# Keys and queries fetched early into the second weight's tile, regrouped joins, more unread products in the chain, and the first MLP group in free order

## The chip, the cores and the metric

The kernel runs on one core of a Trainium2 chip. The metric is the time on the device in microseconds (us), the median of several runs. A smaller time is better. Everything is computed in float32. The names of the engines are those of the profile: PE is the tensor engine's matrix product, PEld its weight load, DVE the vector engine, ACT the scalar engine, POOL GpSimd, SP the sync engine, which here only issues transfers.

## The reference, cut to what matters

Two blocks follow each other. The first is a delta rule (a linear attention whose state is corrected at each position), for 4 batches of 8 heads, 768 positions, head size 48:

```python
k_n = k / (np.linalg.norm(k, axis=-1, keepdims=True) + 1e-06)
for t in range(S):
    y[:, :, t] = np.einsum('bhd,bhde->bhe', q[:, :, t], state)
    v_old = np.einsum('bhde,bhd->bhe', state, k_n[:, :, t])
    state = state + beta[:, :, t, None, None] * np.einsum(
        'bhd,bhe->bhde', k_n[:, :, t], v[:, :, t] - v_old)
```

Its output, with the heads laid side by side, is x: 4 x 768 x 384. The second block mixes by a Fourier transform over positions and over the model's width, and then applies an MLP:

```python
u = x + np.real(np.fft.fft(np.fft.fft(x, axis=1), axis=2))
un = (u - mean(u)) / np.sqrt(var(u) + 1e-06)
out = u + np.maximum(un @ w_ch1, 0.0) @ w_ch2      # 384 -> 1536 -> 384
```

The two weights arrive as float64, and the kernel turns them into float32 itself.

## The kernel before, in words

**The delta rule in chunks.** A group g is 128 positions of one batch, all 8 heads: six groups for a batch (NL), 24 in all. For the groups of a round (RL = 4 groups) the kernel makes the products of the keys with themselves (`pre_a`), and from them the inverse of a unit triangular matrix of 32 x 32, for all heads and blocks side by side on the 128 partitions. `invert` (line 313) does this on DVE: one transpose, some small operations for the norms, then for each of 31 columns a product (L372) and a sum (L376), and two transposes (L379, L380). The first two rounds use `invert16` (line 386), which inverts the blocks of 16 only; `join` (line 464) then adds the corner between two such blocks by two sets of small products on PE, the first for `G` by `Gc`, the second for `Y` by `A` and `A` by `Y`, with an ACT copy between them and two DVE sums after them (L485). `pre_q` (line 493) transposes the queries and multiplies them with the keys. `pre_m` (line 524) forms what a step needs (W and U0), and `step` (line 580) moves the state over 64 positions, two steps for a group. Steps depend on each other; everything else only prepares for them.

**The Fourier part** is `fourier` (line 660): it folds x to even and odd halves (L680 to L691, POOL and DVE), multiplies by the tables over the positions (`pf`, L701 copies them to F), and then, in six T steps, multiplies over the width (`pb`) and adds to x, with the mean and variance for the norm (L720 to L735). **The MLP** is `mlp` (line 741): three groups of 256 positions for a batch. For a group PE makes 12 tiles of `ph` (the first weight, three products each), which ACT or DVE take through the ReLU to hT (L762, L764), and then two tiles of `po` (the second weight, 12 products each), which DVE adds to x (L774). `mlp` is a generator; a unit of it is one `ph` tile or four `po` products.

**The weights.** `weights` (line 221) brings each weight in six pieces, as pairs of 32-bit words. A piece goes through ACT (L253, L261), five operations on DVE (L254 to L265) and a product on POOL (L268), which writes it into w1 or w2.

**Where data lives.** Keys in the layout of `pre_a` have three tiles C and, for groups 3 and 4, the two query tiles. `home` (line 141) says which. Keys 5 to 7 go to the C tiles again, so `pre_a` of groups 0 to 2 issues their transfers when it has read a tile (line 295). Queries have two tiles, `Qs`; `pre_a` of groups 3 and 4 issues the first two, and each `pre_q` issues the query two groups ahead once it has read its own (line 504). `load_beta` issues four small transfers on SP.

**What sets the order.** All of the first batch runs in a block with a hand order (`manual_schedule`): there each engine runs its instructions in the order in which the program writes them. Generators are advanced by hand: `advance(gen, n)` runs n of a generator's units, `drain` the rest. After that block the loop over batches goes on, and there a scheduler orders the instructions. In the block: the keys of the first eight groups, the first inversion, queries 1 to 3, the joins, and then the steps of the six groups, with joins, the second inversion and w1's pieces between (`fill`); then the Fourier part of batch 0, the first group of its MLP with w2's pieces (`conv`), then the third inversion's first instruction, `pre_q(6)` and the beginning of `pre_m(6)`. In the loop, for each later step, `beside` (from line 808) names what runs next to it: the next group's preparation, keys and inversion of the next round, and MLP units of the batch before.

**Unread products.** `spin(n)` (line 195) issues n products of a zero tile with itself, 128 x 128 x 128, into a PSUM tile that nothing reads. In float32 each is two records in the trace. They are there to keep PE busy. The tile of zeros is filled on DVE at the start.

Of the kernel before, what the change touches and what calls it, by code (L numbers as in the profile page):

```python
# [9 lines left out]
F32 = mybir.dt.float32  # L10
# [50 lines left out]
def kernel(  # L61
# [80 lines left out]
    def home(g):  # L142

        return Cs[g] if g < 3 else Qs[g - 3] if g < 5 else Cs[(g - 5) % 3]
# [4 lines left out]

    def load_q(g):  # L150
        if g < NLT:
            nc.sync.dma_start(out=Qs[g % 2][:, :, 0:D], in_=rows(q, g))
# [9 lines left out]
    def load_beta(r):  # L162
# [5 lines left out]
        while i < RL:  # L168
            b, n = divmod(RL * r + i, NL)
            m = min(RL - i, NL - n)  # L170
            for q4 in range(4):
# [4 lines left out]
                nc.sync.dma_start(out=t[p0:p0 + 8 * m], in_=src)  # L176
# [3 lines left out]
    pack = const.tile([128, 128 + C + 3], F32, name="pack")  # L180
    load_c(0)
    nc.scalar.dma_start(out=pack, in_=cn["pack"].ap())
    load_c(1, nc.scalar)
    load_c(2)
    load_c(3)
    load_c(4)
    load_beta(0)
# [19 lines left out]
    w2 = const.tile([128, KF, DM], F32, name="w2")  # L207
# [77 lines left out]
    def pre_a(g):  # L285
# [9 lines left out]
        if g < 3:  # L295
            load_c(g + 5)
        elif g < 5:
            load_q(g - 3)
        else:
            load_c(g + 3)  # L300
# [161 lines left out]
    def join(g):  # L462
# [14 lines left out]
        for m in range(8):  # L477
            for q4 in range(4):
                rw = slice(W * q4, W * q4 + W)
                mm(pm[rw, V16 * m:V16 * m + V16], Y[rw, m, :], MTd[rw, 8 * li + m, V16:W], m == 0)  # L480
                o = 8 * V16 + V16 * m
# [9 lines left out]
    def pre_q(g, QT=None, LQ=None):  # L491

        Q, KT = Qs[g % 2], KTs.pop(g)
# [10 lines left out]
        load_q(g + 2)  # L504
# [340 lines left out]
    with tc.manual_schedule(engines=engines):  # L845
        unread.append(ps_post([128, 512], "unread"))
        spin(18)
# [7 lines left out]
        for g in range(2 * RL):  # L855
            if g == RING:
                drain(qs[0])
            advance(keys[g])
            if g > 0:
                advance(keys[g - 1])  # L860
            if g == RL:
                advance(inv0, 3)
                load_kv(0, nc.gpsimd)
                load_beta(1)
        drain(keys[-1])
        advance(inv1)
        load_kv(1, nc.gpsimd)
        drain(inv0)
        load_kv(2)
# [4 lines left out]
        nc.sync.dma_start(out=dtab, in_=cn["dtab"].ap())  # L874
        for qg in qs[1:4]:
            spin(3)
            advance(qg)
            spin(3)
            drain(qg)
        spin(4)  # L880
# [7 lines left out]
        advance(js[0])  # L888
        advance(js[1])
        advance(inv1, 6)  # L890
        advance(js[2])
        advance(pms[0])
        advance(inv1, 6)
        advance(pms[1])
        advance(pms[0])
        advance(inv1, 6)
        advance(js[2])
        advance(inv1, 6)
        advance(pms[1])
# [15 lines left out]
        for g in range(NL):  # L915
# [5 lines left out]
            if g > 0:  # L921
                advance(s0)
                fill()
                advance(out_g)
# [4 lines left out]
            fill()  # L929
            if g == 1:  # L930
# [5 lines left out]
            spin(2)  # L936
            advance(s1)
            fill()
            advance(p2)
# [4 lines left out]
            if g < NL - 1:  # L944
                advance(s1)
                fill()
                advance(p1)
                for jg in jn:
                    advance(jg)
# [77 lines left out]
```

## Time and profile before

The median of three runs is 855.03 us (852.42 to 860.65); the profiled execution spans 849.1 us.

| What | us | Share |
|---|---|---|
| PE busy | 743.0 | 88% |
| PE weight load busy | 579.4 | 68% |
| DVE busy | 385.1 | 45% |
| ACT busy | 206.2 | 24% |
| POOL busy | 128.7 | 15% |
| `ph` products (864) | 219.3 | |
| `po` products (576) | 197.7 | |
| Mean granted clock of PE | 0.885 of full | |

A busy time is the sum of an engine's instructions in the trace. The share tells how full an engine is over the whole span, and hides that the stages differ. The granted clock is the share of full speed that PE was allowed. In a row of the timeline the first number is the start, the second the time from the first start to the last end of the records gathered in the row; the brackets at its end give the idle time ahead of it on its engine, and after the arrow what ended it. A row of a group of instructions has, after the number of records, the busy time in us and the mean ns of one, and then the idle time ahead of them.

### The profile page before, as it was taken

The page shows a single profiled execution, that of the slowest core. Times are in us where ns is not written, and L with a number is a line of the kernel's source. Part 1 is how long each engine was busy: PE and PEld are TensorE (multiplying, and loading weights), DVE is VectorE, ACT ScalarE, POOL GpSimd, SP SyncE. Part 2 cuts the span into 40 slices and gives each one's busy share as a digit, 9 for nine tenths or more (in the row PEclk, how much of TensorE's full clock was granted, in tenths as well). Part 3 has the DMA queues.
Part 4 walks back from the last instruction along what each step waited for, and adds up shares of the span by engine and source line. Part 5 has one row for each costly group of instructions (what it writes and reads, how often), then busy time and mean ns, then how long its engine had stood idle before and what let it go on. Part 6 is the DMA issues. An engine that isn't in the chain of part 4 may idle for free.

```text
span 849.1 us, 26492 instructions
## 1 busy us (share of the span) xinstructions
PE 743.0 (88%) x11988; PEld 579.4 (68%) x11988; DVE 385.1 (45%) x959; ACT 206.2 (24%) x478; POOL 128.7 (15%) x151
## 2 busy tenths in 40 slices
PE   7658888666579899979998999889999999999998
PEld 6547777555456676748885776767867767776775
DVE  1816444535579611992628812499412131421110
ACT  4213332242231332203331222212212211110010
POOL 3521222201230110112100112101100010000000
PEclk9665555597689999999999999999999999989999
DMA  7911323141212132111211122001111000000000
GB/s 108 221 27 33 70 67 101 25 113 37 77 45 59 28 60 51 36 22 30 53 33 37 40 38 50 14 4 34 30 34 30 2 21 1 19 1 19 5 15 19
DMA packets 107395, 36.28 MB, mean 43 GB/s; under 512 B 99633, under 2 KB 102930, under 8 KB 107282
## 3 DMA queue, kind: packets, MB, share of 16 engines
q1 hardware_dynamic: 105586, 33.50, 17.8%
q8 instruction: 94, 1.54, 0.8%
q0 software_dynamic: 512, 0.79, 0.5%
q10 hardware_dynamic: 1184, 0.30, 0.2%
q14 instruction: 19, 0.16, 0.1%
HBM read 29.84 MB, written 4.72 MB: 41 GB/s over the span
## 4 chain that ended last, share of the span: by engine, by line
PE 60%; DVE 24%; issue 5%; POOL 4%; ACT 4%; DMA 2%; SPq 0%; POOLq 0%; DVEq 0%; ACTq 0%
PE ph L106 17%; PE po L106 16%; PE pair L106 10%; PE one L106 8%; DVE M L376 5%; DVE tmp L372 5%; PE pf L106 3%; PE one L109 3%; PE unread L197 2%; DMA Q<-in_q_dram 2%; POOL w L268 1%; PE pb L106 1%; PE ptr L109 1%; DVE A L379 1%; POOL E L680 1%
## 5 line engine op out<-in xcount | busy, mean ns | idle before, releaser
L106 PE MATMUL ph<-unT,w 128*128 128x256 f32 x864 | 219.3, 408 | 26.5 <-DVE x L725 11.8
L106 PEld LDWEIGHTS ph<-unT,w 128*128 128x128 f32 x864 | 170.2, 203 | 58.0 <-ACT Q L720 9.8
L106 PE MATMUL po<-w,hT 128*128 128x384 f32 x576 | 197.7, 493 | 2.5 <-DVE hT L764 2.4
L106 PEld LDWEIGHTS po<-w,hT 128*128 128x128 f32 x576 | 107.2, 191 | 68.8 <-DVE hT L764 2.6
L764 DVE TENSOR_SCALAR hT<-ph 128x256 f32<-128x256 f32 x72 | 30.3, 421 | 112.6 <-PE ph L106 112.6
L762 ACT ACTIVATE hT<-ph 128x256 f32<-128x256 f32 x72 | 27.5, 382 | 139.5 <-PE ph L106 139.4
L774 DVE TENSOR_TENSOR x<-x,po 128x384 f32<-128x384 f32 x24 | 13.2, 551 | 97.2 <-PE po L106 97.2
L530 POOL TENSOR_TENSOR V<-V,nT 128x384 f32<-128x384 f32 x24 | 21.3, 888 | 187.3 <-DMA V<-in_v_dram 75.7
L106 PE MATMUL one<-V,MT 64*64 64x48 f32 x768 | 46.1, 238 | 1.2 <-issue 0.7
L372 DVE TENSOR_TENSOR tmp<-A,M 128x31 f32<-128x31 f32 (+15 forms) x124 | 44.6, 359 | 3.5
L106 PE MATMUL pair<-MT,K 64*64 64x64 f32 x768 | 42.7, 257 | 3.1 <-issue 2.7
L376 DVE TENSOR_TENSOR M<-M,tmp 128x31 f32<-128x31 f32 (+15 forms) x124 | 43.6, 352 | 3.3
L534 POOL TENSOR_TENSOR MT<-A,pack 128x512 f32<-128x512 f32 x24 | 24.7, 1038 | 131.3 <-PE one L106 83.9
L106 PEld LDWEIGHTS one<-V,MT 64*64 64x64 f32 x768 | 42.5, 156 | 2.5 <-issue 1.4
L106 PEld LDWEIGHTS pair<-MT,K 64*64 64x64 f32 x768 | 39.0, 151 | 5.0 <-issue 4.3
L106 PEld LDWEIGHTS pb<-dtab,F 97*128 97x128 f32 (+1 forms) x192 | 26.9, 211 | 6.5 <-DVE x L774 2.7
L106 PE MATMUL pb<-dtab,F 97*128 97x97 f32 (+1 forms) x192 | 28.8, 300 | 2.9 <-DVE x L774 2.3
L613 DVE TENSOR_TENSOR S<-S,pair 128x192 f32<-128x192 f32 x40 | 14.0, 350 | 37.5 <-PE pair L106 37.4
L558 ACT ACTIVATE MT<-one 32x256 f32<-32x256 f32 x48 | 17.9, 373 | 52.0 <-PE one L106 44.3
L106 PEld LDWEIGHTS pair<-U,K 64*64 64x64 f32 x704 | 17.2, 153 | 18.9 <-issue 9.7
L106 PE MATMUL pair<-KT 48*32 48x64 f32 x1536 | 22.3, 236 | 8.6 <-issue 5.3
L594 DVE TENSOR_TENSOR U<-U,pair 128x192 f32<-128x192 f32 x44 | 15.4, 351 | 30.5 <-PE pair L106 27.8
(148 smaller groups left out, 1035.8 us busy)
## 6 DMA issues: line engine op xcount, KB each, us to landing
w<-in_moe_w_ch_dram SPq DMA_DIRECT2D x12, 768.0 KB
Q<-in_q_dram SPq DMA_DIRECT2D x24, 192.0 KB
out_dram<-x SPq DMA_DIRECT2D x24, 192.0 KB
K<-in_k_dram SPq DMA_DIRECT2D x88, 48.0 KB
V<-in_v_dram SPq DMA_DIRECT2D x88, 48.0 KB
C<-in_k_dram SPq DMA_DIRECT2D x21, 192.0 KB
evt<-k_even SPq DMA_DIRECT2D x1, 579.0 KB
odt<-k_odd SPq DMA_DIRECT2D x1, 576.0 KB
```

What stands on the lines that cost most here:

```text
L106: nc.tensor.matmul(o, lhsT=lhsT, rhs=rhs, start=start, stop=stop, skip_group_check=True)
L109: nc.tensor.matmul(o, lhsT=src, rhs=ident[0:src.shape[0], 0:src.shape[0]], is_transpose=True, start=start, stop=True, skip_group_check=True)
L197: nc.tensor.matmul(unread[0][:, 0:128], lhsT=idle, rhs=idle, start=True, stop=True, skip_group_check=True)
L372: nc.vector.tensor_tensor(t, A[:, j + 1:W, j:j + 1].broadcast_to([128, n, j + 1]), M[:, j:j + 1, 0:j + 1].broadcast_to([128, n, j + 1]), o ...
L376: nc.vector.tensor_tensor(M[:, j + 1:W, 0:j + 1], M[:, j + 1:W, 0:j + 1], t, op=ALU.add)
L530: nc.gpsimd.tensor_tensor(V.rearrange("p c j d -> p (c j) d"), V.rearrange("p c j d -> p (c j) d"), nT[:, m8, None].broadcast_to([128, 8, ...
L534: nc.gpsimd.tensor_tensor(MT, MTd[:, m8, None, :].broadcast_to([128, 8, 2, W]), m_blk[:, None, :, None].broadcast_to([128, 8, 2, W]), op=A ...
L558: nc.scalar.activation(MT[rw, :, 1, :], py[rw, 0:8 * W].rearrange("p (m s) -> p m s", s=W), ACT.Copy)
L594: nc.vector.tensor_tensor(U.rearrange("p (jj jp) e -> p jp jj e", jp=2), U.rearrange("p (jj jp) e -> p jp jj e", jp=2), pw[:, :, 0:2 * D]. ...
L613: nc.vector.tensor_tensor(s1v, s0.rearrange("p h j e -> p h (j e)"), pk, op=ALU.add)
L762: nc.scalar.activation(hT[:, fc, :], ph, ACT.Relu)
L764: nc.vector.tensor_scalar(hT[:, fc, :], ph, 0.0, None, op0=ALU.max)
```

## The change

The change has four parts.

1. **Early fetch.** w2's tile is free until w2's pieces are written. A view of it, `early`, has nine slots of the form of a key tile; keys 5 to 7 take slots 0 to 2 and queries 0 to 5 slots 3 to 8. One DVE memset, ahead of that of the zero tile, clears the padding columns. All eight keys and query 0 are issued at the start, queries 1 to 5 once the keys' products are written in the program, and none has to wait for a tile to come free. Betas are issued from the GpSimd queue instead of SP. Each key's products are also completed sooner after its transposes. It is to take the waits for keys and queries from the start.
2. **Joins.** In the second half of `join` the four row tiles are gone round with one product and then with the other, instead of both products for each tile.
3. **Unread products.** Nine instead of 18 at the start, some one by one between the keys, and more in the chain from the joins to the Fourier part, where they are to hold the granted clock up. Between the first join and the Fourier part 14 become 43; ahead of the joins 40 become 37.
4. **The MLP in free order.** The hand order ends after the T steps. Those have, as before, two MLP units beside each, but no pieces of w2. The rest of the first MLP group, w2's pieces, the third inversion and the query and the matrices of group 6 are left to the scheduler. They are to fill each other's gaps.

```diff
@@ -141,15 +141,18 @@
 
     def home(g):
 
-        return Cs[g] if g < 3 else Qs[g - 3] if g < 5 else Cs[(g - 5) % 3]
+        return Cs[g] if g < 3 else Qs[g - 3] if g < 5 else early[g - 5] if g < 8 else Cs[g % 3]
 
     def load_c(g, engine=None):
         if g < NLT:
             (engine or nc.sync).dma_start(out=home(g)[:, :, 0:D], in_=rows(k, g))
 
+    def home_q(g):
+        return early[3 + g] if g < NL else Qs[g % 2]
+
     def load_q(g):
         if g < NLT:
-            nc.sync.dma_start(out=Qs[g % 2][:, :, 0:D], in_=rows(q, g))
+            nc.sync.dma_start(out=home_q(g)[:, :, 0:D], in_=rows(q, g))
 
     def load_kv(g, engine=None):
         if g < NLT:
@@ -159,7 +162,7 @@
 
     betas = {}
 
-    def load_beta(r):
+    def load_beta(r, engine=None):
 
         if r * RL >= NLT:
             return
@@ -173,18 +176,24 @@
                 p0 = q4 * W + i * 8
                 src = beta[b, 4 * hh:4 * hh + 4, n * L:(n + m) * L].rearrange(
                     "j (c b t) -> b c j t", b=2, t=W)[blk]
-                nc.sync.dma_start(out=t[p0:p0 + 8 * m], in_=src)
+                (engine or nc.sync).dma_start(out=t[p0:p0 + 8 * m], in_=src)
             i += m
         betas[r] = t
 
     pack = const.tile([128, 128 + C + 3], F32, name="pack")
+    w2 = const.tile([128, KF, DM], F32, name="w2")
+
+    early = w2.rearrange("p c m -> p (c m)").rearrange("p (n h d) -> p n h d", h=8, d=64)
+    nc.vector.memset(early[:, :, :, D:64], 0.0)
+    early = [early[:, i] for i in range(9)]
     load_c(0)
     nc.scalar.dma_start(out=pack, in_=cn["pack"].ap())
     load_c(1, nc.scalar)
-    load_c(2)
-    load_c(3)
-    load_c(4)
-    load_beta(0)
+    load_beta(0, nc.gpsimd)
+    for i in range(2, 7):
+        load_c(i)
+    load_q(0)
+    load_c(7)
     ident = pack[:, 0:128]
 
 
@@ -204,7 +213,6 @@
     odt = const.tile([128, TH, 2 * NO], F32, name="odt")
     dtab = const.tile([ND + 1, 4, ND + 1], F32, name="dtab")
     w1 = const.tile([128, KD, DFF], F32, name="w1")
-    w2 = const.tile([128, KF, DM], F32, name="w2")
 
     low_e = const.tile([128, 1], F32, name="low_e")
     nc.gpsimd.memset(low_e, -896.0)
@@ -292,11 +300,7 @@
             tr(pt[:, 128 * i:128 * i + 128],
                K[:, 2 * i:2 * i + 2, :].rearrange("p h d -> p (h d)"), i == 0)
         nc.scalar.activation(KT.rearrange("p h j t -> p (h j t)"), pt, ACT.Copy)
-        if g < 3:
-            load_c(g + 5)
-        elif g < 5:
-            load_q(g - 3)
-        else:
+        if g >= 2 * RL:
             load_c(g + 3)
         yield
         if li == 0:
@@ -478,6 +482,8 @@
             for q4 in range(4):
                 rw = slice(W * q4, W * q4 + W)
                 mm(pm[rw, V16 * m:V16 * m + V16], Y[rw, m, :], MTd[rw, 8 * li + m, V16:W], m == 0)
+            for q4 in range(4):
+                rw = slice(W * q4, W * q4 + W)
                 o = 8 * V16 + V16 * m
                 mm(pm[rw, o:o + V16], MTd[rw, 8 * li + m, :], Y[rw, m, 0:V16], False)
         for t, s0, o in ((Md, 0, 8 * V16), (MTd, V16, 0)):
@@ -490,7 +496,7 @@
 
     def pre_q(g, QT=None, LQ=None):
 
-        Q, KT = Qs[g % 2], KTs.pop(g)
+        Q, KT = home_q(g), KTs.pop(g)
         early = QT is not None
         if QT is None:
             QT = wk.tile([128, 2, 2, 128], F32, tag="QT", bufs=2, name="QT")
@@ -501,7 +507,8 @@
             tr(pt[:, 128 * i:128 * i + 128],
                Q[:, 2 * i:2 * i + 2, :].rearrange("p h d -> p (h d)"), i == 0)
         nc.scalar.activation(QT.rearrange("p h j t -> p (h j t)"), pt, ACT.Copy)
-        load_q(g + 2)
+        if g >= NL:
+            load_q(g + 2)
         yield
         pl = ps_pair()
         for i in range(4):
@@ -844,7 +851,7 @@
                mybir.EngineType.Pool}
     with tc.manual_schedule(engines=engines):
         unread.append(ps_post([128, 512], "unread"))
-        spin(18)
+        spin(9)
 
 
         QT6 = wk.tile([128, NL, 2, 2, 128], F32, tag="F", name="QT6")
@@ -854,30 +861,41 @@
         qs = [pre_q(g, QT6[:, g], LQ6[:, g]) for g in range(NL)]
         for g in range(2 * RL):
             if g == RING:
+                advance(qs[0])
+                drain(keys[g - 1])
                 drain(qs[0])
             advance(keys[g])
             if g > 0:
-                advance(keys[g - 1])
+                drain(keys[g - 1])
+            spin(1)
             if g == RL:
                 advance(inv0, 3)
                 load_kv(0, nc.gpsimd)
-                load_beta(1)
+                load_beta(1, nc.gpsimd)
         drain(keys[-1])
         advance(inv1)
+        for g in range(1, 4):
+            load_q(g)
         load_kv(1, nc.gpsimd)
+        load_q(4)
+        load_q(5)
+        load_kv(2)
         drain(inv0)
-        load_kv(2)
         side = weights()
         advance(side)
         nc.sync.dma_start(out=evt, in_=cn["even"].ap())
         nc.sync.dma_start(out=odt, in_=cn["odd"].ap())
         nc.sync.dma_start(out=dtab, in_=cn["dtab"].ap())
+        for g in range(2 * RL, 2 * RL + 3):
+            load_c(g)
+        load_q(NL)
+        load_q(NL + 1)
         for qg in qs[1:4]:
-            spin(3)
+            spin(2)
             advance(qg)
-            spin(3)
+            spin(2)
             drain(qg)
-        spin(4)
+        spin(8)
 
         js = [join(g) for g in range(2 * RL)]
         pms = [pre_m(g) for g in range(NL)]
@@ -886,16 +904,21 @@
         advance(inv1)
         spin(2)
         advance(js[0])
+        spin(1)
         advance(js[1])
+        spin(2)
         advance(inv1, 6)
         advance(js[2])
         advance(pms[0])
+        spin(2)
         advance(inv1, 6)
         advance(pms[1])
         advance(pms[0])
+        spin(2)
         advance(inv1, 6)
         advance(js[2])
         advance(inv1, 6)
+        spin(1)
         advance(pms[1])
         advance(pms[0])
         advance(inv1, 8)
@@ -921,32 +944,37 @@
             if g > 0:
                 advance(s0)
                 fill()
+                spin(1)
                 advance(out_g)
                 if g == NL - 1:
                     advance(f)
             advance(p2)
             advance(s0)
             fill()
+            spin(1)
             if g == 1:
                 drain(inv1)
             for jg in jn:
                 advance(jg)
             if g in (0, 1):
                 advance(qs[g + 4])
-            spin(2)
+            spin(1)
             advance(s1)
             fill()
+            spin(1)
             advance(p2)
             if g in (0, 1):
                 drain(qs[g + 4])
             if g == NL - 1:
                 advance(f)
-            if g < NL - 1:
+            else:
                 advance(s1)
                 fill()
+                spin(1)
                 advance(p1)
                 for jg in jn:
                     advance(jg)
+                    spin(1)
                 if g == NL - 2:
                     advance(f)
                 load_kv(g + 3)
@@ -968,28 +996,21 @@
         advance(side)
         for _ in range(4):
             advance(f)
-            advance(side)
-            advance(conv, 3)
-            advance(side)
-            advance(conv, 3)
+            advance(side, 2)
             done += 2
         done += 1
-        while done < 13:
-            advance(side)
-            advance(conv, 3)
-            done += 1
-        drain(conv)
-        inv = invert(2)
-        advance(inv)
-        drain(pre_q(NL))
-        pm = pre_m(NL)
-        advance(pm)
+    inv = invert(2)
     for b in range(B):
         if b > 0:
             run([(fourier(b), 1), (side, 1)])
+        if b > 0:
             side, done = mlp(b), 0
         if b + 1 < B:
             if b == 0:
+                run([(part(side, 13 - done), 1), (conv, 3)])
+                done = 13
+                pm = pre_m(NL)
+                drain(pre_q(NL))
                 drain(pm)
             for n in range(2 * NL * (b + 1), 2 * NL * (b + 2)):
                 run([(step(*divmod(n, 2)), 1)] + beside(n))
```

## The prediction

> **What bounds the kernel now.** I read the page's slices first, then the timeline of the first 52 us, then the windows by stage.
>
> ```profile
> PE   7658888666579899979998999889999999999998
> ...
> PEclk9665555597689999999999999999999999989999
> DMA  7911323141212132111211122001111000000000
> ```
>
> A slice is 21.2 us. TensorE (PE) is nearly full from slice 12 on, at full clock. The first twelve slices, about 255 us, are neither full nor fast: there lies what the change can win. The timeline of this head:
>
> ```profile
> 17.03 1.98 DVE L409 STREAM_TRANSPOSE A<-G 128x1024 f32<-128x1024 f32 x1 [16.04 <-ACT G L318]
> ...
> 37.61 0.17 DVE L458 STREAM_TRANSPOSE nT<-nrm 128x32 f32<-128x32 f32 x1
> 47.03 1.09 PE L109 MATMUL one<-pack,Q 128*128 128x128 f32 x4 [9.42 <-DMA Q<-in_q_dram]
> 51.79 0.31 PEld L106 LDWEIGHTS one<-G,Gc 16*32 16x32 f32 x28
> ```
>
> The first inversion runs on VectorE (DVE) from 17.03 to 37.78. The joins need it, but start only at 51.79: PE stood 9.42 us waiting for a query. PE's order is fixed, and the products for queries 1 to 3 lie ahead of the joins. Query 3 can't be fetched until query 1 has left one of two tiles.
>
> Then the stages, by windows (length; busy of PE, weight load, DVE, ACT, POOL; granted clock; DMA share; GB/s):
>
> ```profile
> 52.00:164.00 112.00, 84.63 (x3059) 77.77 (x3045) 54.96 (x128) 33.15 (x65) 28.12 (x25) 0.53 0.25 57
> 164.00:184.00 20.00, 16.81 (x324) 14.39 (x320) 6.42 (x14) 8.17 (x20) 1.81 (x1) 0.84 0.41 115
> 184.00:247.00 63.00, 37.97 (x216) 29.32 (x217) 36.37 (x77) 17.93 (x33) 13.39 (x12) 0.76 0.17 52
> 247.00:288.00 41.00, 37.02 (x600) 25.61 (x592) 38.62 (x96) 8.53 (x20) 8.43 (x9) 0.96 0.22 46
> 288.00:340.00 52.00, 51.44 (x1091) 38.96 (x1092) 10.17 (x21) 16.82 (x40) 4.90 (x6) 1.00 0.25 49
> ```
>
> From 52 to 164 PE works at half clock (0.53). From 184 to 247 no engine is full: PE 38 of 63, DVE 36. From 247 to 288 DVE is full (38.6 of 41): the third inversion. After that PE has no gap. The third inversion waits, by the hand order, for the whole conversion of w2:
>
> ```profile
> 246.31 1.82 POOL L268 TENSOR_TENSOR w<-wtmp 128x768 f32<-128x768 f32 x1 [5.16 <-DVE wtmp L265]
> 246.48 1.98 DVE L331 STREAM_TRANSPOSE A<-G 128x1024 f32<-128x1024 f32 x1
> ...
> 285.92 2.00 DVE L380 STREAM_TRANSPOSE G<-M 128x1024 f32<-128x1024 f32 x1
> ```
>
> **What the Trainium skill says.** "TensorE: Matmul & The Clock Gate", part 1: the clock is full or half, decided in free-running windows of 3413 ns from how busy PE was. The trace agrees: the granted clock changes only at multiples of 3.413 us (down at 20.6, up at 34.25, down 41.07, up 51.3, down 58.1). "Runtime: NRT & Kernel Launch", Instruction fetch mechanics: PE's instructions come in blocks of 256, and crossing a block is mostly hidden. Here the trace differs. In dense small products the 16 KB packets of queue q8 come 3.35 to 3.9 us apart (57.32, 61.23, 65.14, 69.0, 72.87), and the waits name "issue" at the weight loads:
>
> ```profile
> PEld one L106 <- issue: 9.9, 8, 2.4
> ```
>
> A waiting time of up to 2.4 us for nothing else. "DMA: Bandwidth & Descriptors", Issuing engines are not separate DMA queues: issuing on another engine saves only sequencer time. The trace agrees: SyncE is held 3.45 us by four beta transfers from 4.68, and the next key goes out only at 8.48.
>
> **The change part by part.**
>
> **Early fetch.** Keys 5 to 7 and queries 0 to 5 get homes in w2's tile, and are issued at the start. A 192 KB transfer takes 1.15 to 1.2 us alone on the queue, so nine more end by about 25 us, and no query waits for a tile. Then two things decide where the joins start. First the start of PE: unread products run from 1.04 to 8.01 now, nine records' worth too long, for the first transposes at 7.85 follow them and key 0 landed at 3.5. Nine leave instead of 18, each 0.387 us: 3.5 us. They wait for one added DVE memset of 9 x 8 x 16 = 1152 elements. No row shows it; below it is a DVE row of 0.17 us, above it one element per cycle at 0.96 GHz ("VectorE: DVE Perf Modes", memset section), an estimate of 1.2 us. I take 1.1: spins from 2.1 to 5.6. The key chain then starts 2.3 us earlier; the inversion starts at about 14.9 and ends at 35.6, its 20.7 us being DVE's own. Second, PE: without the 9.42 us wait, it is ready at 29 to 31, so the inversion is the bound. The joins start near 36.3 instead of 51.8: **-15.5** (14 to 17). The moved beta issue costs POOL's queue some issue slots while it has only memsets: nothing.
>
> **Order within joins.** The same 1024 products in rounds over the four row tiles, not alternating. Both products' rows show the same 203 and 206 ns, start to start about 13 ns cold, and instruction fetch holds them anyway. Nothing.
>
> **Unread products.** Before the joins 40 become 37. In the chain from joins to fold 14 become 43. The row is two records each:
>
> ```profile
> L197 PE MATMUL unread<-idle 128*128 128x128 f32 x28 | 7.7, 427 | 0.0
> ```
>
> So 0.55 us each at half clock; in fully clocked stretches, half. They add 29 x 0.55 = 16 us at most, 8 at least. The chain of waits from 52 to 164 has 4.6 of the 7.7 us on it, 60%; the rest lies in waits for DVE, ACT or fetch. So 5 to 10 us on the path. What they buy is clock. The same product is quicker there: first row 52 to 164, second 300 to 690, at full clock:
>
> ```profile
> L106 PE MATMUL one<-V,MT 64*64 64x48 f32 x192 | 17.1, 300 | 0.7 <-issue 0.7
> ...
> L106 PE MATMUL one<-V,MT 64*64 64x48 f32 x480 | 24.0, 217 | 0.5 <-ACT MT L558 0.3
> ```
>
> That is 89 against 50 ns a record. But would the clock rise? I weighed each window of 3.413 us by the array area times the columns of its products, a full-array product of 128 columns being 128. The clock rose after windows with 1475 or more and stayed low up to 1322. A step of the chain (17.5 us, 5.1 windows) holds 2560 of work; with two unread products (256 each, both records) some 600 a window, with five 820, the first two steps 925 to 1155. That is short of 1350 on average; only the densest windows (1208, 1224, 1322 in the trace) plus one unread product cross it. I take a few warm windows, worth 4 to 6 us, against 5 to 10 us of cost: **+2**. The bounds: clock full throughout, where fetch is the floor: 24.8 blocks x 3.55 us = 88 against 105 us, so -17; and no gain with all on the path, +16.
>
> **MLP in free order.** The first MLP group, w2's conversion, the third inversion and its query leave the hand order. The T steps of the Fourier part go ahead of the rest with two MLP steps each. Built, DVE's order has the six w2 pieces from instruction 192 to 304, with the inversion's start and 9 of its 31 steps between; before, the inversion followed all pieces. From DVE instruction 368 on the orders are the same. Now the pieces end on POOL at 203.46, 213.78, 222.79, 232.17, 239.34 and 246.31: 8.57 us apart on average, 7.0 at best, since DVE interleaves them with Fourier steps and each waits ACT and POOL in turn; DVE is idle 27 of 63 us. With the inversion to fill those gaps (each step needs only DVE), I expect the pieces' end 55 us after the fold's products end (184.2 now; 50 to 62), and 22 steps and two transposes later, 26 us, plus about 4 for the waits, the inversion's end at 85, up to 95. Now it is 287.9 - 184.2 = 103.7. **-12** (8 to 17). The wait added: the first `po` products wait for w2's last piece, and on PE the step products queue behind them; with pieces no later than now it costs nothing, later up to 16 us (two pieces). PE also has 16 `ph` products' groups already done when the inversion ends, of 0.408 us, in a stretch that PE bounds (51.4 of 52): 6.5, of which I take **-5**.
>
> Sum: 855 - 15.5 + 2 - 12 - 5 = 824.5, so **825**.
>
> **The rivals.**
> **A**, as above: 825, chance 0.50.
> **B**, the clock stays up through the chain. For: windows close to the threshold. Against: 820 a window on average. Then -17 in place of +2: 825 - 19 = **806**, chance 0.22.
> **C**, the free order gains little, as w2's pieces set the end and the pieces compete with the inversion, and the products cost more than they give: 855 - 15.5 + 10 - 3 = **846**, chance 0.20. For: DVE has 36 + 39 us of work here whatever the order. Against: its 27 idle us.
> **D**, slower: the early gain is partly lost (-10) as the fetches delay each other, the unread products lie wholly on the path at half clock (+16), and PE, in order, stands at `po` for late w2 pieces (+8): 855 + 14 = **869**, chance 0.08. Against: the 9.42 us wait is shown and its cause removed.
>
> **How the numbers follow.** The time is A's. B reaches to about 803 and C to 848, which together with A leaves out D and the tails: range **803 to 848**. Faster by over 1% is below 846.5: A, B and half of C, **0.82**; within 1%: the rest of C and part of D, **0.12**; slower **0.06**.
>
> **What would show it.** The joins' first product near 36 and no wait of PE on Q above 1 us; the first inversion still 20.7 us long. The granted clock between joins and fold: near 0.55 to 0.65 for A, above 0.85 for B. The "unread" row 86 records long there, and its share of the chain of waits. w2's last POOL piece some 55 us after the fold's products, the third inversion's last transpose 85 to 95 after. A join start later than 42, a clock that falls below 0.53, or an inversion that ends as far from the fold as now would each make the prediction wrong.

## The result, and the profile after

The changed kernel takes 831.98 us (median of four runs, 826.71 to 841.5) against 856.26 us before (852.42 to 860.65): a ratio of 0.969, 95% interval 0.962 to 0.977. The ratio leaves out the execution of 841.5 us, over 1.5% above the fastest. The forecast was 825, range 803 to 848. The two traces span 849.1 and 830.6 us, 18.5 apart.

The page's slices after, each 20.8 us:

```profile
PE   8789999689978899899998998899999999999998
...
PEclk9755555596999999989998999999999999889999
```

Slices count from 0. PE is fuller from the start, and from slice 12 on it is nearly full at nearly full clock; the stretch at half clock is still there in slices 2 to 7. The timeline of the head, after:

```profile
16.67 2.00 DVE L413 STREAM_TRANSPOSE A<-G 128x1024 f32<-128x1024 f32 x1 [14.47 <-ACT G L322]
...
30.10 0.45 PE L106 MATMUL pair<-KT 48*32 48x64 f32 x11 [3.35 <-issue]
...
36.34 1.95 DVE L460 STREAM_TRANSPOSE A<-M 128x1024 f32<-128x1024 f32 x1
...
39.71 2.05 PE L206 MATMUL unread<-idle 128*128 128x128 f32 x16
41.69 1.13 PE L106 MATMUL one<-G,Gc 16*32 16x32 f32 x96
```

No product waits for a query any more. The joins start at 41.69 instead of 51.79. The inversion is over at 38.3; what stands directly ahead of the joins is PE's own unread products, and further ahead 3.35 us put down to "issue", which I read as PE waiting for its instructions (late_loads, below, bears on that).

The windows of after, from the joins to the first T step and from there to the end of the third inversion (columns as above):

```profile
41.69:183.10 141.41, 121.54 (x3503) 105.80 (x3502) 64.48 (x142) 42.12 (x88) 33.66 (x30) 0.59 0.25 60
183.10:267.74 84.64, 76.27 (x833) 57.70 (x824) 75.73 (x176) 26.96 (x54) 18.57 (x16) 0.92 0.23 60
```

The same two stages of before:

```profile
51.79:184.90 133.11, 102.55 (x3445) 93.06 (x3444) 61.39 (x141) 41.90 (x87) 30.14 (x26) 0.58 0.27 66
184.90:287.92 103.02, 74.05 (x743) 54.20 (x734) 74.91 (x172) 25.89 (x51) 21.74 (x20) 0.83 0.18 49
```

The chain from joins to T steps is 8.3 us longer, at the same clock, with 19 us more of busy PE. The stage after it is 18.4 us shorter for the same work of DVE: its 75 us now fill 84.6 us instead of 103. The third inversion no longer stands behind w2 (timeline of after):

```profile
241.37 1.87 POOL L276 TENSOR_TENSOR w<-wtmp 128x768 f32<-128x768 f32 x1 [2.31 <-DVE wtmp L273]
...
265.78 1.96 DVE L384 STREAM_TRANSPOSE G<-M 128x1024 f32<-128x1024 f32 x1
```

Five marks in the traces make the account (us from the start; in brackets the time since the mark before):

| Kernel | joins start | first T step | third inversion ends | fourth inversion ends | first `pf` of batch 1 | end | time (median), ratio |
|---|---|---|---|---|---|---|---|
| before | 51.8 | 184.9 (133.1) | 287.9 (103.0) | 382.6 (94.7) | 392.7 (10.2) | 849.1 (456.4) | 856.3 |
| after | 41.7 | 183.1 (141.4) | 267.7 (84.6) | 358.5 (90.8) | 371.7 (13.3) | 830.6 (458.8) | 832.0, 0.969 |
| early_only | 41.9 | 177.4 (135.5) | 280.5 (103.1) | 379.3 (98.8) | 389.4 (10.2) | 853.6 (464.2) | 848.7, 0.991 |
| free_only | 50.9 | 184.8 (133.9) | 269.6 (84.8) | 357.7 (88.1) | 372.6 (14.9) | 828.7 (456.1) | 831.6, 0.974 |
| old_join | 39.9 | 183.1 (143.2) | 268.7 (85.6) | 360.1 (91.4) | 370.2 (10.2) | 831.6 (461.4) | 836.8, 0.977 |
| chain14 | 41.0 | 175.3 (134.3) | 260.3 (85.0) | 348.1 (87.8) | 363.0 (14.9) | 826.7 (463.7) | 824.7, 0.966 |
| chain14_again | 42.7 | 179.6 (136.9) | 264.6 (85.0) | 352.7 (88.1) | 367.6 (14.9) | 823.9 (456.3) | 825.7, one run |
| chain0 | 41.2 | 174.8 (133.6) | 259.7 (84.9) | 347.6 (87.9) | 357.8 (10.2) | 815.6 (457.8) | 818.9, 0.957 |
| chain_double | 41.2 | 187.8 (146.6) | 272.8 (85.0) | 360.1 (87.3) | 373.4 (13.3) | 828.9 (455.5) | 839.5, 0.980 |
| head0 | 38.1 | 171.5 (133.4) | 256.4 (84.9) | 346.2 (89.8) | 356.4 (10.2) | 822.2 (465.9) | 814.8, 0.953 |
| late_loads | 38.0 | 174.6 (136.6) | 259.1 (84.5) | 347.1 (88.0) | 357.2 (10.2) | 821.2 (464.0) | 825.8, 0.964 |
| lean | 39.7 | 173.1 (133.4) | 258.0 (84.9) | 348.2 (90.2) | 358.4 (10.2) | 817.3 (459.0) | 822.3, 0.957 |
| lean_fill | 38.9 | 176.3 (137.4) | 261.8 (85.5) | 353.8 (92.0) | 364.6 (10.8) | 824.1 (459.5) | 821.2, 0.959 |
| lean_spread | 37.6 | 172.5 (134.9) | 257.1 (84.6) | 345.8 (88.7) | 356.0 (10.2) | 813.4 (457.4) | 819.9, 0.955 |

From before to after: -10.1 to the joins, +8.3 to the first T step, -18.4 to the third inversion's end, -3.9 to the fourth's, +3.1 and +2.5 after that; in all -18.5. Each ratio in the table is against executions of before in the same session, whose medians are 855.1 to 858.0 us. A trace shows one execution: those of early_only (855.4 us) and head0 (824.0) are the longest of their kernel's, that of chain_double (830.7) is its shortest, and that of before (850.9) is shorter than the four timed ones, so the traces of before and after lie 18.5 us apart and the medians 24.3.

### The profile page after: what moved, and what is told of

Read it like the earlier page. It is cut to its first block, busy times and chain, and to the rows that moved or that the text cites. A ratio compares the mean times of both kernels' runs of the same rounds, so it can differ in the third digit from the quotient of the medians.

```text
span 830.6 us, 26585 instructions
## 1 busy us (share of the span) xinstructions
PE 760.7 (92%) x12040; PEld 591.2 (71%) x12040; DVE 387.1 (47%) x960; ACT 206.9 (25%) x478; POOL 136.4 (16%) x163
## 4 chain that ended last, share of the span: by engine, by line
PE 66%; DVE 22%; issue 4%; POOL 3%; ACT 2%; DMA 2%; SPq 0%; POOLq 0%; DVEq 0%; ACTq 0%
PE ph L106 17%; PE po L106 16%; PE pair L106 11%; PE one L106 8%; DVE M L380 4%; PE unread L206 4%; DVE tmp L376 4%; PE pf L106 3%; PE one L109 3%; PE pb L106 2%; PE ptr L109 1%; DVE A L383 1%; DVE G L384 1%; POOL E L688 1%; POOL E L687 1%
## 5 line engine op out<-in xcount | busy, mean ns | idle before, releaser
L106 PE MATMUL ph<-unT,w 128*128 128x256 f32 x864 | 212.2, 399 | 7.2 <-DVE hT L771 3.9
L106 PEld LDWEIGHTS ph<-unT,w 128*128 128x128 f32 x864 | 165.9, 198 | 35.4 <-DVE hT L771 6.6
L769 ACT ACTIVATE hT<-ph 128x256 f32<-128x256 f32 x72 | 27.7, 384 | 153.5 <-PE ph L106 150.5
L206 PE MATMUL unread<-idle 128*128 128x128 f32 x160 | 46.6, 421 | 2.3 <-DVE idle L201 2.3
L206 PEld LDWEIGHTS unread<-idle 128*128 128x128 f32 x160 | 33.4, 280 | 5.9 <-DVE idle L201 2.2
L106 PEld LDWEIGHTS pair<-KT 48*32 48x32 f32 x1536 | 18.2, 112 | 17.0 <-issue 14.3
L601 DVE TENSOR_TENSOR U<-U,pair 128x192 f32<-128x192 f32 x44 | 15.5, 352 | 31.6 <-PE pair L106 31.6
```

Source lines behind the costliest of these rows:

```text
L106: nc.tensor.matmul(o, lhsT=lhsT, rhs=rhs, start=start, stop=stop, skip_group_check=True)
L206: nc.tensor.matmul(unread[0][:, 0:128], lhsT=idle, rhs=idle, start=True, stop=True, skip_group_check=True)
L601: nc.vector.tensor_tensor(U.rearrange("p (jj jp) e -> p jp jj e", jp=2), U.rearrange("p (jj jp) e -> p jp jj e", jp=2), pw[:, :, 0:2 * D]. ...
L769: nc.scalar.activation(hT[:, fc, :], ph, ACT.Relu)
```

## The experiments

### One part alone: early fetch, free order

`early_only` is the kernel before with the new homes, the new order of the head and its loads; `free_only` is the kernel before with the hand order ended after the T steps.

```diff
--- before
+++ early_only
-        return Cs[g] if g < 3 else Qs[g - 3] if g < 5 else Cs[(g - 5) % 3]
+        return Cs[g] if g < 3 else Qs[g - 3] if g < 5 else early[g - 5] if g < 8 else Cs[g % 3]
...
--- before
+++ free_only
-            advance(side)
-            advance(conv, 3)
-            advance(side)
-            advance(conv, 3)
+            advance(side, 2)
...
+                run([(part(side, 13 - done), 1), (conv, 3)])
```

> Only the early fetch with its head of the program (keys, queries, betas, nine unread products at the start); joins, chain and MLP as before. Theory: joins start near 41.7 as in the changed kernel, the stretch to the first T step is 132 us as before, and the 10 us stay to the end: 856 - 10 = 846. Rival (the gain is given back, for something later was waiting anyway, such as w1's conversion or the third inversion): 852 to 857.

Measured: ratio 0.991 (0.988 to 0.994), 848.7 us. The theory's 846 lies within this interval, the rival's 852 does not. The joins start at 41.9 as expected; the first T step comes 7.5 us sooner than before, since the stretch between is 2.4 us longer, which two traces of one kernel can differ by (below).

> Only the MLP group, w2's conversion and the third inversion in free order; everything ahead of it as before. Theory: the third inversion ends about 18 us sooner after the first T step (85 us instead of 103), and the kernel takes 856 - 18 = 838, down to 835 with the MLP products done meanwhile. Rival (the free order gains only because the chain ahead of it changed, or is lost again where PE is full): 848 to 857.

Measured: ratio 0.974 (0.967 to 0.980), 831.6 us: alone it brings nearly all that the whole change brings. Its window from the first T step to the third inversion's end is that of after to within 0.3 us:

```profile
184.80:269.70 84.90, 76.38 (x828) 57.77 (x824) 76.04 (x176) 26.89 (x54) 18.42 (x16) 0.92 0.22 60
```

It gained 18.1 us there, and 6.6 more up to the end of the fourth inversion (88.1 instead of 94.7), which I had not expected from this part alone to that size; 4.7 of these are lost again on the way to the next `pf` (14.9 instead of 10.2).

### The unread products

`chain14` is the changed kernel with the 14 unread products of before between joins and T steps instead of 43; `chain0` has none there, `chain_double` 86.

```diff
--- after
+++ chain14
         advance(js[0])
-        spin(1)
         advance(js[1])
-        spin(2)
...
-            spin(1)
+            spin(2)
             advance(s1)
             fill()
-            spin(1)
...
                 for jg in jn:
                     advance(jg)
-                    spin(1)
```

> The changed kernel with the unread products between the first join and the Fourier part as they were before (14 instead of 43); all else changed. Theory (they cost more path than they save in fetch gaps; the clock is not their doing): from the first join to the first T step 132 us instead of 141, unread on the chain of waits near 5 us instead of 22, issue near 20 instead of 9, clock there still near 0.53; time 832 - 8 = 824. Rival 1 (they pay through the clock or the fetch): the stretch stays at 141 or grows, time 832 to 840. Rival 2 (another part of the change has made the stretch longer): 141 with few unread products, time 832.

Measured: 824.7 us, ratio 0.966 (0.960 to 0.972), the stretch 134.3 us. The lines below are the chain of waits in this stretch by line, first before, then after, chain14 and chain_double (shares of 133.1, 141.4, 134.3 and 146.6 us):

```profile
by line: PE one L106 27.4%; PE pair L106 20.2%; issue 16.6%; PE pf L106 7.8%; PE unread L197 3.6%; PE one L109 3.2%; POOL w L268 2.7%; POOL E L681 1.7%; POOL E L680 1.5%; DVE man L256 1.4%; ACT man L253 1.4%; DVE x L643 1.3%; ACT x L634 1.0
```

```profile
by line: PE one L106 26.9%; PE pair L106 21.3%; PE unread L206 15.6%; PE pf L106 6.9%; issue 6.6%; PE one L109 3.0%; POOL w L276 2.6%; DVE man L264 1.7%; DVE num L273 1.3%; DVE num L262 1.3%; DVE O L694 1.3%; DVE E L692 1.2%; DVE O L691 1.1
```

```profile
by line: PE one L106 27.5%; PE pair L106 23.3%; issue 14.5%; PE pf L106 8.2%; PE unread L206 4.4%; PE one L109 3.2%; POOL w L276 2.7%; DVE man L264 1.4%; ACT man L261 1.4%; POOL MT L541 1.0%; ACT x L641 1.0%; DVE E L692 0.8%; DVE O L691 0.8
```

```profile
by line: PE one L106 22.8%; PE unread L206 22.6%; PE pair L106 19.1%; issue 7.3%; PE pf L106 7.0%; PE one L109 2.9%; POOL w L276 2.5%; DVE E L692 1.7%; DVE man L264 1.3%; DVE num L273 1.3%; ACT man L261 1.2%; DVE O L691 1.1%; DVE x L650 0.8
```

From chain14 to after, unread goes from 5.9 to 22.1 us (+16.2) and issue from 19.5 to 9.3 (-10.2); the rest changes by 1.1. But "issue" in this chain is not PE's alone: 3.03 us of it in chain14, at 140.61, is a wait of POOL. PE's own waits on "issue" in the two stretches, first in chain14, then in after:

```profile
PE one L106 <- issue: 9.3, 7, 2.3
PE pair L106 <- issue: 5.2, 5, 1.6
```

```profile
PE one L106 <- issue: 7.4, 7, 1.6
```

They fall from 14.5 to 7.4 us, by 7.1. So an unread product costs its time, and PE's shorter waits for instructions give back some 45% of it. That the next block of instructions has time to come while it runs would explain this, and is not shown. The clock is 0.59 in both. The added products bought no clock. Across all kernels, the stretch is between 133.1 and 137.4 us in all eleven traces with 0 to 14 of these products, and 141.4 and 143.2 in the two with 43.

> The changed kernel with twice the unread products between the first join and the Fourier part (86 instead of 43). Theory (cost on the path, fetch gaps already filled for the most part): 43 x 0.55 us x 75% = 18 us less up to 6 us of the 9 us of issue left: 832 + 12 = 844, clock below 0.65 there. Rival (a threshold of the clock is crossed and the stretch runs at full clock): clock over 0.85 there, the stretch down to 125 us, time near 816.

Measured: 839.5 us, ratio 0.980 (0.972 to 0.988). The stretch is 146.6 us, unread 33.1 us of it, issue still 10.7. The window gives a mean clock of 0.70, over the theory's 0.65 and far under the rival's 0.85:

```profile
41.19:187.80 146.61, 124.44 (x3590) 110.13 (x3589) 64.59 (x142) 41.99 (x88) 33.32 (x30) 0.70 0.25 60
```

Here the clock does rise in part, and all but unread and issue falls from 110.0 us in after (77.8% of 141.4) to 102.8. That doesn't pay for the products either: with 86 of them the stretch is still 5.2 us longer than with 43. How busy PE must be for the clock to stay up is not shown by these runs.

> The changed kernel without any unread product after the joins begin (0 instead of 43, chain14 has 14). Theory (each costs 0.28 us of path net of the fetch gaps it fills, by 8 us for 29): 14 fewer give another 4 us, first T step at 171.5 instead of 175.5, time 821. Rival (the first 14 stand where PE waits anyway, for DVE or ACT, or for fetch): 174 to 176, time 825.

Measured: 818.9 us, ratio 0.957 (0.950 to 0.963), but the first T step is at 174.8, only 0.5 us sooner than in chain14. The rival holds for the stretch: the first 14 cost nothing there that shows. Its time of 825 is not reached, as 818.9 lies under the theory's 821 too. The further 10.6 us of its trace against chain14's lie in later stages, nearly all of them where the clock falls in one trace and not in the other (below); the intervals of the two kernels overlap.

### The head: why the joins start at 41.7 and not at 36

`head0` is chain14 without the 20 unread products around the queries.

```diff
--- chain14
+++ head0
         for qg in qs[1:4]:
-            spin(2)
             advance(qg)
-            spin(2)
             drain(qg)
-        spin(8)
```

> The kernel of chain14 without the 20 unread products that stand between the queries and ahead of the joins. Theory (in the changed kernel PE, not the first inversion, sets the start of the joins, and the first half of a join needs only the inverse itself, there at 34.3, not its transposes, done at 38.3): the joins start 5 to 7 us sooner, at 35 to 36.5 instead of 41.3, the first T step as much sooner, and the time is 825 - 5 = 820. Rival (the clock, which these products hold up, falls and the joins lose what was won; or the second halves wait for the transposes): joins start sooner but the first T step not by more than 2 us, time 823 to 829.

Measured: 814.8 us, ratio 0.953 (0.946 to 0.961). The joins start at 38.1, 2.9 us sooner, and the first T step is 3.8 us sooner. One pair of traces is thin ground, since chain14's own two lie 1.7 and 4.3 us apart at these marks; but the joins start at 39.9 to 42.7 in all seven traces of the early fetch with these 20 products and the same transfers, and at 38.1 to 39.7 in the three without them (head0, lean, lean_fill). They don't start at 35 to 36.5, for PE is late without unread products too. Its timeline in this kernel:

```profile
37.00 1.13 PE L106 MATMUL pair<-QT,KT 48*64 48x64 f32 x32 [0.69 <-ACT QT L509]
38.07 1.93 PE L106 MATMUL one<-G,Gc 16*32 16x32 f32 x128
```

PE goes from the last query's products to the joins without a wait. The first join starts before the transpose of M to A ends at 38.5, so its first half does not need that transpose.

`late_loads` is chain14 with the Fourier tables and the first two pieces of w1 held back: DVE writes one column of each after the first inversion, and the transfers wait for that.

```diff
--- chain14
+++ late_loads
+                if i == 0:
+                    nc.vector.memset(ring[:, :, 0:1, :], 0)
                 stage(i)
                 stage(i + 1)
...
+        for t in (evt[:, 0, 0:1], odt[:, 0, 0:1], dtab[:, 0, 0:1]):
+            nc.vector.memset(t, 0.0)
```

> The kernel of chain14 with the Fourier tables and the first two pieces of w1 held back until the first inversion is done (one column of each is written by DVE there, and the transfer waits for that). Theory (PE's instruction blocks queue behind the data of the head's transfers): the wait of PE on issue of 4.2 us near 25 to 29 shrinks to under 2, the joins start 2 to 3 us sooner at about 39, while new issue waits appear where the held-back transfers now run, after 38; time 822 to 826. Rival (the fetch is slow by itself, whatever the queues hold): the wait stays 3 to 4 us, joins at 41, time 825.

The wait ahead of the same 11 products in the timelines, first in chain14, then in late_loads, with late_loads' longest wait after it:

```profile
29.43 0.45 PE L106 MATMUL pair<-KT 48*32 48x64 f32 x11 [4.21 <-issue]
```

```profile
28.39 0.33 PE L106 MATMUL pair<-KT 48*32 48x64 f32 x11 [0.93 <-issue]
...
45.76 0.24 PE L106 MATMUL one<-Y,A 32*32 32x16 f32 x3 [4.45 <-issue]
```

The wait falls from 4.21 to 0.93 us and a new one of 4.45 us stands where the transfers went, in the joins. But late_loads also comes to these products 2.2 us later (27.46 instead of 25.22), so that PE goes on only 1.04 us sooner. From there to the joins it takes 9.6 us instead of 11.6, at full clock (22.8 to 43.3), where chain14 is at half clock from 27.7 to 34.6.

The traces also record PE's instruction packets, 16 KB each on queue q8, and these show the cause more directly. A packet takes 0.9 to 1.9 us in every trace. But the fourth starts 7.7 us after the third in chain14, and 6.6 to 8.1 us after it in all ten traces of the early fetch that have these transfers there; in the two that hold them back it is 4.2 us (late_loads) and 5.1 us (lean_spread, below). Where late_loads has them instead, the sixth and the seventh packet are 6.7 us apart, in chain14 4.0. So PE's next instructions start on their way later beside these transfers; what holds them back there is not shown.

The joins start 3.0 us sooner, and the stretch after them is 2.3 us longer: 825.8 us, ratio 0.964, the time of chain14.

### The order within the joins

```diff
--- after
+++ old_join
                 mm(pm[rw, V16 * m:V16 * m + V16], Y[rw, m, :], MTd[rw, 8 * li + m, V16:W], m == 0)
-            for q4 in range(4):
-                rw = slice(W * q4, W * q4 + W)
                 o = 8 * V16 + V16 * m
```

> The changed kernel with the joins' second half in the old order, both products for each row tile in turn. Theory (no effect, the products are held by instruction fetch either way): the first join's second half takes the same within 0.3 us, time 832, within 4. Rival (rounds over the tiles overlap better): each second half is 0.5 us longer or more, the first T step 4 us later, time 836.

Measured: 836.8 us, ratio 0.977 (0.971 to 0.983), an interval that overlaps that of after. This is the time that the rival names, but the traces do not bear it out. The first T step is at 183.1 in both. In the third and fourth join, where PE waits for nothing, the second half (128 records) takes 1.91 and 1.90 us in after, 1.97 and 1.96 in old_join. At 0.06 us a join, the eight joins give 0.5 us in all, not 4. What else lies between the two medians is open.

### Where two traces of one kernel differ

> The kernel of chain14 unchanged, profiled a second time. In its first trace the clock fell to half near 349 to 356 and near 560 to 571, at waits of PE for DVE of 1.8 and 1.3 us. Theory (whether it falls there depends on how the free-running windows happen to lie): at one of the two places at least the clock does not fall this time, and that stretch is 4 to 6 us shorter. Rival (the falls belong to this kernel's order of work): the same two falls at the same instructions.

In both traces the clock falls near 350, after PE's wait of 1.8 us for the fourth inversion, and the way to the next `pf` is 14.9 us instead of 10.2. chain0 has the same wait, 1.75 us, and no fall, so the wait alone does not bring it. Near 560 it falls in the first trace only. The timeline there, of chain14's first and second trace:

```profile
559.30 2.93 PE L106 MATMUL pb<-dtab,F 97*128 97x97 f32 x16 [1.26 <-DVE x L781]
```

```profile
561.48 2.03 PE L106 MATMUL pb<-dtab,F 97*128 97x97 f32 x16 [1.25 <-DVE x L781]
```

The same instructions behind the same wait take 2.93 or 2.03 us. From the first T step of batch 2 to the end of the sixth inversion it is 28.2 us (549.1 to 577.3) in the first trace and 22.6 (551.3 to 573.9) in the second. The theory holds for one of the two places; that the lie of the windows decides is not shown. In chain0 the clock falls at neither, which gives it 4.7 and 5.5 us on chain14. So a difference of 5 us in one trace says nothing of the change. The marks before that spread too: in the second trace the joins start 1.7 us later and the first T step comes 4.3 us later. From the T step to the end of the third inversion the two agree, at 85.0 us.

### Versions without unread products

`lean` is the changed kernel without any unread product from the queries on, so head0 without its last 14. `lean_fill` adds unread products at the two places just named; `lean_spread` holds back the tables, w1's pieces and later keys until into the chain, one after another.

```diff
--- lean
+++ lean_fill
         px = ps_one()
+        if g in (3 * RL, 4 * RL):
+            for _ in range(4):
+                nc.tensor.matmul(px[:, 0:128], lhsT=ident, rhs=ident, start=True, stop=True,
...
+            if b == 2 and T > 2:
+                pz = ps_one()
+                for _ in range(3):
+                    nc.tensor.matmul(pz[:, 0:128], lhsT=ident, rhs=ident, start=True, stop=True,
...
--- lean
+++ lean_spread
+        advance(side)
+        tables = iter(((evt, "even"), (odt, "odd"), (dtab, "dtab")))
...
+            if 0 < g < 4:
+                t, name = next(tables)
+                nc.vector.memset(t[:, 0, 0:1], 0.0)
+                nc.sync.dma_start(out=t, in_=cn[name].ap())
```

> The changed kernel without any unread product from the queries on: neither the 20 ahead of the joins nor the 43 after. Early fetch, join order and free order stay. Theory (unread products cost path in both places and buy no clock): joins start at 38, first T step 171 to 172, time 814 to 818. Rival (without any, the clock stays low into the Fourier part and the T steps): first T step 175 or later, time 822.

> The kernel of lean with unread products at two other places only: four ahead of the first product that waits for an inversion (rounds 3 and 4, where PE waits 1.75 us for DVE), and three ahead of each of the last three T steps of batch 2. Theory (at these two places a window of the clock falls under its threshold or not, by where it happens to lie, and a fall costs 3 to 6 us each): no fall of the clock near 345 to 375 and 557 to 575, the runs spread less, the median 2 to 5 us under lean. Rival (the falls have another cause or the added 3 to 4 us of products cost as much): median within 2 us of lean or above.

> The kernel of lean with the transfers of w1's first pieces, of the Fourier tables and of the keys and queries of later rounds held back until into the chain, one after another. Theory (PE's instruction blocks queue behind data, so data spread thin costs less of it): the wait on issue near 25 to 29 under 1.5 us, none over 2.5 us at the joins, joins start 2 us sooner at 36, first T step 2 to 3 us sooner than lean, time 2 to 3 us less. Rival (spread data delays the blocks of the dense chain instead, or w1 comes too late): first T step not sooner, time the same or up to 6 us more.

Measured: 822.3, 821.2 and 819.9 us, ratios 0.957 (0.953 to 0.961), 0.959 (0.955 to 0.962) and 0.955 (0.951 to 0.959). The three can't be told apart. lean's first T step is at 173.1, between what theory and rival say, and its time is the rival's 822, 4 us over the theory's. In lean_fill's trace the clock stays up near 560 (22.4 us from T step to inversion), but so it does in lean's (22.6), so the added products are not shown to do it, and the time is the same: its rival stands. lean_spread started the joins 2.1 us sooner and came to the first T step only 0.6 us sooner. Its wait ahead of the 11 products is 2.30 us, against 2.61 in lean and the 1.5 that the theory allows; PE goes on 2.35 us sooner there (28.43 instead of 30.78). Its waits at the joins were up to 1.96 us, although no data moves there. head0, lean and lean_spread beat both kernels: their intervals lie wholly under that of after (0.962 to 0.977). So the change is faster without most of its unread products.

## Why the prediction was right, and where its steps were not

The time was 7 us over the forecast and within the range. Three terms gave less than forecast, early fetch by 5.4 us, unread products by 5 to 6 and PE's stretch by 4.2, and one, the free order, gave 6.4 more. That the sum came so near is in part luck: early fetch and free order both lie outside the ranges that I had given them.

- **Early fetch, -15.5: measured -10.1.** The step that failed is "PE: without the 9.42 us wait, it is ready at 29 to 31, so the inversion is the bound". PE is ready at 41.7 and is the bound. The timeline of before already said so: without its wait PE would have come to the joins at 51.79 - 9.42 = 42.4. I left out two things that lay in PE's own row: the 20 unread products still ahead of the joins, worth 2.9 us in head0's trace, and its waits for instructions, 1.51, 1.46 and 3.35 us in after's timeline, the last of which shrinks when the transfers beside it go (late_loads). The inversion started at 16.67 rather than 14.9: the nine unread products at the start took 4.21 us, not 3.5, and four between the first keys, of 0.5 to 0.6 us each, had been put at nothing. The memset took 1.02 us, against the estimate of 1.2 and the 1.1 taken. A join start later than 42 was named as a sign of being wrong; 41.7 is just short of it, and chain14's second trace, at 42.7, is past it. The direction, the removed wait and the length of the inversion (16.67 to 38.3, 21.6 us against 20.7) were right.
- **Unread products, +2: measured +7 to +8.** Case A's step was right that the clock stays low, and B is refuted: clock 0.59, two windows at full clock between 52 and 164. The term that failed is "a few warm windows, worth 4 to 6 us". They gave nothing that shows: chain14, without the added products, has two as well ahead of the Fourier part. The threshold is not borne out. Weighed in the same way, the windows before these four have some 1190 and 1170 (after), 880 and 1060 (chain14), all under 1322, while others of up to 1356 and 1232 in the same two stretches left the clock low. The cost of "5 to 10 us on the path" was right in sum, though not in its parts: 16 us more on the chain, 7 us less of PE's waits for instructions and 3 us less of a wait of POOL.
- **Joins, nothing:** holds for the joins themselves, to 0.06 us each.
- **MLP in free order, -12: measured -18.4** (and -18.1 alone). The mechanism was right; the size was off, and already in the sum: 55 + 26 + 4 is 85, which is 18.7 less than 103.7, and I entered 12. The end at 85 then came about through two errors that cancel. The pieces' end came 61 us after the fold's products, at the late end of the 50 to 62 given, but the inversion needed only 24.5 us from there instead of 26 + 4. The times that I gave as the pieces' ends were their starts; by their ends the last piece came 63.9 us after the fold's products before and 60.8 now. So the conversion is hardly sooner. What moved is the inversion, which took 39.8 us from there before. The new wait, `po` for w2's last piece, is 1.45 us at 243.29.
- **PE's stretch, -5: measured -0.8** to the next `pf`. Up to the fourth inversion 3.9 us were gained (6.6 in free_only); of these 3.1 were lost again in a fall of the clock near 360.
- **C** came near the cost of the products, 10 us, and had the free order wrong. **D** is refuted by the time. Its early gain of 10 us is the one measured, but the products cost half of its 16, and the wait at `po` is 1.45 us and not 8.

## What to carry to other kernels

When a wait on an in-order engine is taken away, add up everything that still stands ahead of the next work on that engine, its filler products and instruction fetch included, before another engine is named as the bound. A filler product meant for the clock has to show in the granted clock, or it only costs (here 7 us, at 0.59 with it and without); test it by leaving it out. Before a mark in one trace is credited to a change, take a second trace of the same kernel and see how far the mark moves. Work that needs one engine alone is best let into the gaps of a chain that goes through three engines, rather than put behind it.

## What the runs showed of the hardware that I had not expected

PE's instruction packets start later beside large data transfers: the same two packets were 6.6 to 8.1 us apart in ten traces with the transfers there and 4.2 and 5.1 us in two without, and two later ones 6.7 us apart where the transfers had been moved to, against 4.0. Unread products shorten PE's waits for instructions by some 45% of their own time: 7.1 us for 16.2. One wait of PE of 1.25 us is followed by a fall of the clock that costs 5.5 us in one execution of a kernel, and by none in another.
